# Two of the last four row tiles kept in PSUM, the last softmax in one bank, and a new instruction order

## The chip, the cores and the metric

The kernel runs on one core of a Trainium2 chip. The metric is device time in microseconds (us) of that core; a comparison is between medians of several runs. The profiler takes one execution of the program apart, and its own time is given beside its span.

## What is computed

```python
def reference(A_x, A_wqkv, A_wo, B_x, B_W_gate, B_W_up, B_W_down):
    ...
    x = A_x                                   # 1 x 2048 x 512, bf16
    xn = _layernorm(x, axis=-1)
    return x + _A_ref(xn, A_wqkv, A_wo) + _B_ref(xn, B_W_gate, B_W_up, B_W_down)
```

A is multi-head attention over 2048 tokens with 32 heads of 16 columns: the product with wqkv gives q, k and v, then per head softmax(q k^T / 4) v, then the product with wo. B is a gated layer: (relu(xn W_gate) * (xn W_up)) W_down, with 1792 columns in the middle. The input x is added to the sum of both.

## The kernel before

**Stages.** Queries are taken in four column groups of 512 (`c4` = 0 to 3), heads in four groups of eight (`gg`), and each group of eight in two halves of four heads (`ee`). A block (c4, gg, ee) goes over 16 key tiles of 128. Its raw scores come out of TensorE transposed, keys on the partitions. For most key tiles ScalarE makes the exponential: one unit is an ACTIVATE of 128 x 1024 scores in two PSUM banks (line 1721), and there are 704 units. For the other key tiles ("quads") VectorE, and POOL behind it, build the exponential out of integer arithmetic (lines 1682, 1696, 1699). The weighted sums with v are products into one PSUM bank per block ("PV", `pv_stream`, line 1641); a column of ones in v gives the sum of the exponentials as one more row. `normalise` divides by it: copy out (1544), sums by a small transfer (1562), reciprocal (1583), back by a transfer (1585), spread over the partitions (1597), product (1600).

The gated layer, the projections of q and k and the output rows run between these units as further chains of products (`mm_chain`). An output row tile is 128 tokens x 512 columns: `out_rows` sums the products with W_down (14 pairs) and with wo (one pair per head group) into one bank.

**TensorE's unit of work.** Nearly all products are issued as halves: four matmuls that use 64 of the 128 rows of the array and 32 columns each (`chain_part`, line 1099). Half 0 and half 1 use different rows and can run side by side. Where two halves of one bank follow each other, `follow` (lines 632 to 636) makes the later one wait for the earlier:

```python
if e == "PE" and o.half is not None:
    was = last.get(o.bank)
    if was is not None and was.half != o.half:
        o.deps[was] = True
    last[o.bank] = o
```

**PSUM.** Eight banks: two pairs for the scores of the units (`P_sc`), and four single banks (`P_b`) for everything else: raw scores of quads, PV, row tiles, projections.

**The order.** The order of the instructions on all five queues is written out by hand: `ORDER` (line 154) is a list of the numbers that the instructions get as they are made, and `SLOTS` (line 471) gives the buffers in the same order. `follow` walks both lists, `emit` adds the semaphore waits. Transfers are issued by SP alone, in the order of the list, but for one store that ScalarE issues at the end (`OWN_STORE`).

**The end.** The last four row tiles (c4 = 3, rows 0 to 3) can't wait for the last head group, so `out_rows` sums what is there (14 pairs and two head groups), and VectorE adds x and puts the result into SBUF as fp32 (`resid`, line 1379). The last block (3, 3, 1) is the only one whose PV halves go to two banks (`LAST2` = 1, lines 1612 to 1621), `tp` for half 0 and `tp_hi` for half 1. `normalise_last` (line 1444) then works in two rounds of 256 columns: ScalarE copies `tp` (1471), VectorE adds `tp_hi` (1473), transposes blocks of 32 x 32 (1476) so that the sums lie along a row, takes the reciprocal (1477), transposes it back, broadcast over 32 columns (1478), and multiplies (1480). TensorE meanwhile sums the missing head groups of the four rows into the four score banks (`stream_out`): group 2, the first half of group 3, and, as soon as a round is done, the second half of group 3 (called the finals below). VectorE adds `resid` to rows 0, 1 and 2 while it empties them (1499). For row 3 an fp32 product with an identity matrix (1455) adds `resid` in the bank, and ScalarE empties it (`TAIL_ACT`, 1495). Four stores end the program (1509, 1506).

## Time and profile before

| | before |
|---|---|
| runs: median (lowest to highest of 3) | 672.91 us (672.89 to 673.71) |
| the profiled execution: its own time | 672.07 us |
| the profiled execution: its span | 670.3 us |
| granted TensorE clock, mean | 1.000 |
| DMA: share of the 16 engines' span, main queue | 15.2% |

The span runs from the first to the last instruction of one execution. A row of a group gives line, engine, operation, output and input, shapes and count, then busy time in all and the mean of one in ns, then the idle time of the engine just before these instructions and what ended it. A row of a timeline gives start, length, engine, line and operation, with the number of instructions merged in it, and in brackets the wait before it. Lengths of merged rows run from the first start to the last end. Matmul ends are modelled. PE is TensorE, ACT ScalarE, DVE VectorE, POOL GpSimd, SP SyncE; a q behind the name is the engine's queue of transfers.

### The profile page before, as it was taken

The page shows a single profiled execution, that of the slowest core. Times are in us where ns is not written, and L with a number is a line of the kernel's source. Part 1 is how long each engine was busy: PE and PEld are TensorE (multiplying, and loading weights), DVE is VectorE, ACT ScalarE, POOL GpSimd, SP SyncE. Part 2 cuts the span into 40 slices and gives each one's busy share as a digit, 9 for nine tenths or more (in the row PEclk, how much of TensorE's full clock was granted, in tenths as well). Part 3 has the DMA queues.
Part 4 walks back from the last instruction along what each step waited for, and adds up shares of the span by engine and source line. Part 5 has one row for each costly group of instructions (what it writes and reads, how often), then busy time and mean ns, then how long its engine had stood idle before and what let it go on. Part 6 is the DMA issues. An engine that isn't in the chain of part 4 may idle for free.

```text
span 670.3 us, 44373 instructions
## 1 busy us (share of the span) xinstructions
PE 662.2 (99%) x22332; PEld 368.4 (55%) x19124; DVE 594.4 (89%) x1001; ACT 656.3 (98%) x721; POOL 334.4 (50%) x345
## 2 busy tenths in 40 slices
PE   8999999999999999999999999999999999999997
PEld 3555465555554555555555555555554556565653
DVE  8958899999999888999999788999999967889887
ACT  7999999999999999999999999999999999999995
POOL 3101445555555654564665544664446644545550
PEclk9999999999999999999999999999999999999999
DMA  6530210122320011111100011020200003020101
GB/s 197 82 42 21 53 44 7 37 57 67 93 73 16 6 48 50 35 54 32 29 21 17 10 51 49 21 77 5 61 6 14 9 26 102 21 80 19 29 5 43
DMA packets 51472, 28.66 MB, mean 43 GB/s; under 512 B 18840, under 2 KB 50328, under 8 KB 51288
## 3 DMA queue, kind: packets, MB, share of 16 engines
q1 hardware_dynamic: 51144, 25.70, 15.2%
q8 instruction: 162, 2.65, 1.7%
q14 instruction: 22, 0.18, 0.1%
q10 hardware_dynamic: 144, 0.13, 0.1%
HBM read 18.22 MB, written 2.10 MB: 30 GB/s over the span
## 4 chain that ended last, share of the span: by engine, by line
PE 89%; ACT 7%; DVE 3%; issue 0%; DMA 0%; POOL 0%; DVEq 0%
PE ps L547 88%; ACT ring L1721 7%; DVE stats L1011 1%; DVE qd L1682 0%; DVE xn_sb L1034 0%; DMA x_sb<-in_A_x_dram 0%; DVE xnT L1079 0%; DVE xn_sb L1499 0%; PE ps L1107 0%; DVE x_sb L1600 0%; DVE mv L1013 0%; DVE o_sb L1476 0%; DVE up_sb L1478 0%; DVE o_sb L1473 0%; DVE xnT L1379 0%
## 5 line engine op out<-in xcount | busy, mean ns | idle before, releaser
L1721 ACT ACTIVATE ring<-ps 128x1024 bf16<-128x1024 f32 x704 | 648.3, 1084 | 2.2 <-PE ps L547 1.5
L1696 POOL INT64_ADD qd<-qd x312 | 321.5, 1044 | 290.8 <-DVE qd L1682 142.8
L547 PE MATMUL ps<-qT,kT 64*32 64x512 bf16 x8192 | 462.2, 375 | 1.4 <-ACT ring L1721 0.5
L1682 DVE TENSOR_SCALAR qd<-ps 128x512 int16<-128x512 f32 x640 | 417.4, 686 | 41.8 <-PE ps L547 35.2
L547 PE MATMUL ps<-qd,v_aug 64*32 64x512 bf16 x3840 | 264.7, 375 | 0.0
L547 PE MATMUL ps<-ring,v_aug 64*32 64x512 bf16 x2816 | 228.7, 375 | 0.2 <-issue 0.2
L1661 PEld LDWEIGHTS <-kT 64*32 64x32 bf16 x7332 | 158.6, 92 | 114.5 <-issue 22.8
L1633 PEld LDWEIGHTS <-v_aug 64*32 64x32 bf16 x4308 | 104.0, 92 | 58.3 <-issue 12.0
L547 PE MATMUL ps<-xnT,wus 64*32 64x512 bf16 x1792 | 134.9, 375 | 0.2 <-DVE qd L1682 0.2
L547 PE MATMUL ps<-xnT,wgs 64*32 64x512 bf16 x1792 | 134.4, 375 | 0.0
L547 PE MATMUL ps<-Wd,hT 64*32 64x512 bf16 x768 | 65.5, 375 | 0.0
L1114 PEld LDWEIGHTS <-wgs 64*32 64x32 bf16 x1792 | 43.4, 92 | 30.0 <-issue 6.6
L1114 PEld LDWEIGHTS <-wus 64*32 64x32 bf16 x1792 | 43.5, 92 | 29.1 <-issue 6.2
L1114 PEld LDWEIGHTS <-hT 64*32 64x32 bf16 x1792 | 43.2, 92 | 27.2 <-issue 3.9
L547 PE MATMUL ps<-Wk,hT 64*32 64x512 bf16 x512 | 46.3, 375 | 0.1
L547 PE MATMUL ps<-Wv,hT 64*32 64x512 bf16 x512 | 45.3, 375 | 0.0
L547 PE MATMUL ps<-Wo_p,x_sb 64*32 64x512 bf16 x480 | 41.6, 375 | 0.0
L1335 DVE SCALAR_TENSOR_TENSOR hT<-ps,up_sb 128x512 bf16<-128x512 f32 x56 | 38.2, 683 | 3.5 <-PE ps L547 2.9
L1331 DVE COPY up_sb<-ps 128x512 f32<-128x512 f32 x56 | 38.5, 687 | 3.2 <-PE ps L547 2.9
L547 PE MATMUL ps<-xnT,Wq 64*32 64x512 bf16 x480 | 36.2, 375 | 0.0
L547 PE MATMUL ps<-xnT,Wk 64*32 64x512 bf16 x448 | 33.1, 375 | 0.0
L547 PE MATMUL ps<-Wv,xnT 64*32 64x512 bf16 x512 | 28.1, 375 | 0.5 <-issue 0.3
(83 smaller groups left out, 218.1 us busy)
## 6 DMA issues: line engine op xcount, KB each, us to landing
wus<-in_B_W_up_dram SPq DMA_DIRECT2D x38, 128.0 KB, 2.7
wgs<-in_B_W_gate_dram SPq DMA_DIRECT2D x38, 128.0 KB, 2.8
xr_sb<-in_A_x_dram SPq DMA_DIRECT2D x16, 128.0 KB, 2.6
qT<-qf SPq DMA_DIRECT2D x120, 16.0 KB, 2.4
o_sb<-o_sb SPq DMA_DIRECT2D x60, 32.0 KB, 2.4
out_dram<-xn_sb SPq DMA_DIRECT2D x15, 128.0 KB, 2.4
x_sb<-in_A_x_dram SPq DMA_DIRECT2D x8, 128.0 KB, 2.8
Wd<-in_B_W_down_dram SPq DMA_DIRECT2D x6, 128.0 KB, 3.3
```

The lines of the kernel that those rows point to most:

```text
L547: return e.add_instruction(mybir.InstMatmult(name=e.bass.get_next_instruction_name(), engine=mybir.EngineType.PE, ins=[e.lower_ap(x), e.lo ...
L1011: G.op("DVE", 580, lambda e, m=m: e.bn_stats(stats[:, m, :], xs(m)), reads=[t_xm[m]], writes=[t_st], prio=pr, order=last_xn if m == 4 and ...
L1114: e.ldweights(w()[rows, 32 * j:32 * j + 32], tile_position=(rows.start, 32 * j))
L1331: G.op("DVE", 603, lambda e: e.tensor_copy(up_sb[:, tup.slot, :], bank_of(tu)), reads=[tu], writes=[tup], prio=-590)
L1335: G.op("DVE", 603, lambda e: e.scalar_tensor_tensor(out=hT[:, th.slot, :], in0=bank_of(tg), scalar=0.0, in1=up_sb[:, tup.slot, :], op0=ALU ...
L1633: e.ldweights(vs(j), tile_position=(64 * half, 32 * j))
L1661: e.ldweights(ks(m), tile_position=(64 * half, 32 * m))
L1682: G.op("DVE", 601, lambda e, j=j, tx=tx: e.tensor_scalar(qd[:, tq.slot, 512 * j:512 * j + 512], ps[:, BANK[tx.slot], :], IBIAS[3], 0.0, op ...
L1696: G.op("POOL", POOL_NS, lambda e, x=x, n=n: e.int64_add(x().bitcast(I64), raw().bitcast(I64), SHIFTS[n + 1] * LANES), reads=[ti, tq, t_lib ...
L1721: exp_ops[u] = G.op("ACT", ACT_NS, lambda e, tr=tr, k0=k0: e.activation(ring[:, tr.slot, :, :], ps[:, 4 * k0:4 * k0 + 2, :], ACTF.Exp, sca ...
```

## The change

Rows are made in the order 0, 3, 1, 2. Rows 1 and 2 (`KEEP`) are not emptied by VectorE: their banks (of `P_b`) stay theirs to the end. x is added there by one more pair of the chain, a bf16 identity matrix times the x tile that was loaded for the row (two halves), and the missing head groups are summed into the same bank (`more=6`, and `share`, which hands on the counter that marks the first and the last product of a bank). Their halves need no longer stand behind the last PV. Rows 0 and 3 keep the old way, in one score bank each, and VectorE empties them; ScalarE empties rows 1 and 2 (`TAIL_ACT`), and issues the store of row 2. The fp32 identity product is gone.

The last block's PV goes to one bank (`LAST2` = 0). The softmax transposes this bank in one instruction of 512 columns, takes 16 reciprocals in one, transposes them back in one, and multiplies in two instructions of 256 columns that read the bank. The copies of ScalarE and the additions are gone.

`ORDER` and `SLOTS` are replaced from the third line of `ORDER` on: 8020 instructions in place of 8026. The instructions made ahead of the third row tile keep their numbers; the later ones are shifted by one or two.

```diff
@@ -50,9 +50,10 @@
 POOL_SHARE = 1.0
 POOL1_SHARE = 1.0
 FIRSTD = 2
-LAST2 = 1
+LAST2 = 0
 LASTD = 2
-TAIL_ACT = (3,)
+TAIL_ACT = (1, 2)
+KEEP = (1, 2)
 MUL_SLACK = 2500.0
 PAT_SLACK = 100
 REC_SLACK = 3000
@@ -65,7 +66,7 @@
 XN_WAIT = 0
 SPREAD_NS = 660
 VE_FIRST = True
-OWN_STORE = (3,)
+OWN_STORE = (2,)
 JOB_SHIFT = {2: -1, 6: -4, 9: 3, 13: 4, 14: -1, 33: -1, 34: -4, 36: 2, 41: -2, 47: 1, 49: 4, 50: 1, 51: -4, 53: -1, 59: -9, 71: 2, 72: -4, 73: -1, 75: -2, 78: -2, 79: 3, 80: -1, 83: 5, 84: -4, 88: -1, 89: -1, 92: -1, 97: 4}
 XN_POOL = ()
 XN_NS = 2080
@@ -154,343 +155,342 @@
 ORDER = [
...
-    7791, 7813, 7824, 7978, 7963, 7979, 7971, 7985, 7981, 7994, 7989, 7982, 7986, 7983, 7995, 7987, 7990, 7998, 7999, 8000, 8001, 8002, 8003, 8012, 8013,
-    8014, 8015, 8016, 7996, 7988, 7984, 7997, 7991, 8004, 7992, 8005, 8008, 8017, 8006, 8007, 7993, 8009, 8010, 8011, 8018, 8022, 8019, 8020, 8021, 8023,
-    8024, 8025,
...
+    7988, 7925, 7927, 7698, 7956, 7824, 7992, 7964, 7802, 7700, 7972, 7976, 7979, 7980, 7842, 7843, 7844, 7845, 7990, 7799, 7981, 7999, 7819, 7708, 7993,
+    7996, 7989, 7800, 7983, 7987, 7808, 7701, 7994, 8000, 7717, 7812, 7995, 7820, 7718, 7986, 7795, 7984, 7693, 8001, 8002, 8008, 8004, 7825, 7998, 8007,
+    8009, 8010, 8011, 8012, 8016, 8003, 7985, 7826, 8013, 8005, 8006, 8017, 7822, 7997, 8018, 8019, 7794, 7814, 8014, 8015,
...
@@ -1117,23 +1117,25 @@

         chains = [0]

-        def mm_chain(tile, pairs, reads, prio, sub=0, slots=None, mode="half", weights=None):
+        def mm_chain(tile, pairs, reads, prio, sub=0, slots=None, mode="half", weights=None, more=0, share=None, late=()):

             n = len(pairs)
-            count = [0, n * (2 if mode == "half" else 1)]
+            count = [0, n * (2 if mode == "half" else 1) + more]

             def flags():
                 count[0] += 1
                 return count[0] == 1, count[0] == count[1]
+            if share is not None:
+                share.append(flags)
             made = []
             chains[0] += 1
             for i, (w, x) in enumerate(pairs):
                 at = slots[min(i * len(slots) // n, len(slots) - 1)] if slots else None
                 for half in ((0, 1) if mode == "half" else (None,)):
                     fn, load = chain_part(w, x, lambda: bank_of(tile, sub), half, flags)
-                    G.op("PE", 216, fn, reads=reads, joins=[tile],
+                    G.op("PE", 216, fn, reads=reads + (list(late) if i == n - 1 else []), joins=[tile],
                          prio=prio if prio < 0 else at + BG_PRIO if slots else prio, after=at, mode=mode, half=half, bank=(tile, sub),
-                         load=load, weights=reads if weights is None else weights)
+                         load=load, weights=(reads + (list(late) if i == n - 1 else [])) if weights is None else weights)
                     made.append(G.ops[-1])
             return made

@@ -1346,7 +1348,9 @@

             return xnT[:, i, 0:1024].bitcast(FP32)

-        def out_rows(c4, i, gs, first, last, slots=None, pr=0.0, tile=None, sub=0):
+        kept = {}
+
+        def out_rows(c4, i, gs, first, last, slots=None, pr=0.0, tile=None, sub=0, keep=False):

             t = tile or Tile("ob", P_b, BGBANKS)
             pairs, reads = [], [t_wo]
@@ -1367,6 +1371,12 @@
                 src, rd = xr_sb, [txr]
             else:
                 rd = [t_res[m]]
+            if keep:
+                pairs.append(((lambda: ident[:]), (lambda: xr_sb[:, txr.slot, :])))
+                share = []
+                mm_chain(t, pairs, reads, pr, slots=slots, sub=sub, more=6, share=share, late=[txr, t_id])
+                kept[i] = t, share[0]
+                return
             mm_chain(t, pairs, reads, pr, slots=slots, sub=sub)
             if last:
                 to_ = Tile("ost", P_xn)
@@ -1402,11 +1412,11 @@
         seq, done_h = [], set()
         for c4 in range(NB):
             rows = []
-            for i in range(4):
+            for i in range(4) if c4 < NB - 1 else (0, 3, 1, 2):
                 if c4 < NB - 1:
                     rows.append((upos(c4 + 1) + ROW_AT, RN, lambda s, c4=c4, i=i: out_rows(c4, i, range(4), True, True, slots=s), 2))
                 else:
-                    rows.append((upos(c4 + 1) - 54, RN - 1, lambda s, c4=c4, i=i: out_rows(c4, i, range(2), True, False, slots=s), 2))
+                    rows.append((upos(c4 + 1) - 54, RN - 1, lambda s, c4=c4, i=i: out_rows(c4, i, range(2), True, False, slots=s, keep=i in KEEP), 2))

             todo = [ft for ft in range(0, FT, 2) if (c4, ft) not in done_h]
             both = todo[:(NHS - FT) // 2] if c4 < NB - 1 else []
@@ -1443,62 +1453,47 @@

         def normalise_last(tp, tp_hi):

-            tos = Tile("o", P_o)
-            res_op = {}
             tA, tB = Tile("finA", P_sc, [0]), Tile("finB", P_sc, [1])
-            rows = [(tA, 0), (tA, 1), (tB, 0), (tB, 1)]
+            rows = [(tA, 0), (kept[1][0], 0), (kept[2][0], 0), (tB, 0)]
+            flags = {i: kept[i][1] if i in kept else counted(6) for i in range(4)}
             last = len(G.ops)
             for i in range(4):
                 t, sub = rows[i]
-                if i in TAIL_ACT:
-
-                    o = G.op("PE", 860, lambda e, i=i, t=t, sub=sub: e.matmul(bank_of(t, sub), identf[:], resid(i), start=False, stop=False),
-                             reads=[t_res[12 + i], t_selp], joins=[t], prio=-920, mode="full", after=NU)
-                    res_op[i] = o
                 for n, (tg, wo) in enumerate(((t_oT[(3, 2)], lambda: Wo_p[:, 2, :]), (t_oT[(3, 3)], lambda: Wo_l[:, 0, :]))):
-                    for o in stream_out(t, sub, i, lambda tg=tg, i=i: oT_of(tg)[:, 128 * i:128 * i + 128], wo, [tg], n == 0, False, NU + 5 + i):
-                        o.order |= set(pv_ops[part(keys[-1])][-2:])
+                    for o in stream_out(t, sub, i, lambda tg=tg, i=i: oT_of(tg)[:, 128 * i:128 * i + 128], wo, [tg], n == 0, NU + 5 + i, flags[i]):
+                        if i not in kept:
+                            o.order |= set(pv_ops[part(keys[-1])][-2:])
             tl = Tile("oTl", P_qf)
             oTl = lambda: qf[:, tl.slot, :]
             at_bank = lambda t: ps[:, BANK[t.slot], :]

-            tot, tup = Tile("ot", P_o), Tile("up", P_up)
-            flip = lambda c: o_sb[:, tot.slot, c]
+            tot, tup, tr = Tile("ot", P_o), Tile("up", P_up), Tile()
+            G.op("DVE", 630, lambda e: e.transpose(o_sb[:, tot.slot, :], at_bank(tp)), reads=[tp], writes=[tot], prio=-949)
+            G.op("DVE", 190, lambda e: e.reciprocal(rlast[:], o_sb[:, tot.slot, DH - 1:512:32]), reads=[tot], writes=[tr], prio=-948)
+            G.op("DVE", 630, lambda e: e.transpose(up_sb[:, tup.slot, :], rlast[:].unsqueeze(2).to_broadcast([128, 16, 32])), reads=[tr], writes=[tup], prio=-947)
             half_done, ends = [], []
             for h in range(2):
                 c = slice(256 * h, 256 * h + 256)
-                to, th, tt, tr, ts, tn = (Tile() for _ in range(6))
-                G.op("ACT", 300, lambda e, c=c: e.activation(up_sb[:, tup.slot, c], at_bank(tp)[:, c], ACTF.Copy), reads=[tp],
-                     writes=[th] if h else [tup, th], joins=[tup] if h else [], prio=-950 + h)
-                G.op("DVE", 340, lambda e, c=c: e.tensor_tensor(o_sb[:, tos.slot, c], up_sb[:, tup.slot, c], at_bank(tp_hi)[:, c], ALU.add),
-                     reads=[tp_hi, th], writes=[to] if h else [tos, to], joins=[tos] if h else [], prio=-950 + 10 * h, order=half_done)
-
-                G.op("DVE", 340, lambda e, c=c: e.transpose(flip(c), o_sb[:, tos.slot, c]), reads=[to], writes=[tt] if h else [tot, tt], joins=[tot] if h else [], prio=-949 + 10 * h)
-                G.op("DVE", 190, lambda e, c=c, h=h: e.reciprocal(rlast[:, 8 * h:8 * h + 8], flip(c)[:, DH - 1:256:32]), reads=[tt], writes=[tr], prio=-948 + 10 * h)
-                G.op("DVE", 340, lambda e, c=c, h=h: e.transpose(up_sb[:, tup.slot, c], rlast[:, 8 * h:8 * h + 8].unsqueeze(2).to_broadcast([128, 8, 32])),
-                     reads=[tr, to], writes=[ts], prio=-947 + 10 * h)
-                G.op("DVE", 340, lambda e, c=c: e.tensor_tensor(oTl()[:, c], o_sb[:, tos.slot, c], up_sb[:, tup.slot, c], ALU.mult),
-                     reads=[ts, to], writes=[tn], joins=[tl], prio=-946 + 10 * h)
+                tn = Tile()
+                G.op("DVE", 340, lambda e, c=c: e.tensor_tensor(oTl()[:, c], at_bank(tp)[:, c], up_sb[:, tup.slot, c], ALU.mult),
+                     reads=[tup, tp], writes=[tn], joins=[tl], prio=-946 + 10 * h)
                 half_done = G.ops[-1:]
                 for i in (2 * h, 2 * h + 1):
                     t, sub = rows[i]
                     tf = Tile("fin%d" % i)
-                    if i in res_op:
-                        res_op[i].order.add(fin_prev[(t, sub)])
-                        fin_prev[(t, sub)] = res_op[i]
-                    tf.w += stream_out(t, sub, i, lambda i=i: oTl()[:, 128 * i:128 * i + 128], lambda: Wo_l[:, 1, :], [tn], False, True, -910 + i)
+                    tf.w += stream_out(t, sub, i, lambda i=i: oTl()[:, 128 * i:128 * i + 128], lambda: Wo_l[:, 1, :], [tn], False, -910 + i, flags[i], (1, 0) if i % 2 else (0, 1))
                     t.r += tf.w
                     m = 12 + i
                     to_ = Tile("ost", P_xn)
                     for d in ((slice(0, 512),) if TAIL_ACT or i < 3 else (slice(0, 256), slice(256, 512))):
                         if i in TAIL_ACT:
                             G.op("ACT", 90 + 0.93 * (d.stop - d.start), lambda e, t=t, sub=sub, to_=to_, d=d: e.activation(xn_sb[:, to_.slot, d], bank_of(t, sub)[:, d], ACTF.Copy),
-                                 reads=[tf], writes=[] if to_.w else [to_], joins=[to_] if to_.w else [], prio=-900 + i)
+                                 reads=[tf, t], writes=[] if to_.w else [to_], joins=[to_] if to_.w else [], prio=-900 + i)
                             continue
                         ends.append(to_)
                         G.op("DVE", 70 + 1.04 * (d.stop - d.start), lambda e, i=i, t=t, sub=sub, to_=to_, d=d: e.tensor_tensor(
                             xn_sb[:, to_.slot, d], bank_of(t, sub)[:, d], resid(i)[:, d], ALU.add),
-                             reads=[tf, t_res[m]], writes=[] if to_.w else [to_], joins=[to_] if to_.w else [], prio=-900 + i)
+                             reads=[tf, t, t_res[m]], writes=[] if to_.w else [to_], joins=[to_] if to_.w else [], prio=-900 + i)
                     for k, w in enumerate(to_.w):
                         d = slice(512 // len(to_.w) * k, 512 // len(to_.w) * (k + 1))
                         if i in OWN_STORE:
@@ -1516,20 +1511,22 @@
                     if o.eng == "DVE":
                         o.order.add(half_done[0])

-        def stream_out(t, sub, i, w, wo, reads, start, stop, prio):
+        def counted(n):
+            count = [0]
+
+            def flags():
+                count[0] += 1
+                return count[0] == 1, count[0] == n
+            return flags
+
+        def stream_out(t, sub, i, w, wo, reads, start, prio, flags, halves=(0, 1)):
             made = []
-            for half in range(2):
-                fn, load = chain_part(w, wo, lambda: bank_of(t, sub), half, lambda first=start and not half, last=stop and half: (first, bool(last)))
-                new = not t.w
-                o = G.op("PE", 216, fn, reads=reads + [t_wo, t_wol], writes=[t] if new else [], joins=[] if new else [t], prio=prio, mode="half", half=half,
+            for half in halves:
+                fn, load = chain_part(w, wo, lambda: bank_of(t, sub), half, flags)
+                o = G.op("PE", 216, fn, reads=reads + [t_wo, t_wol], writes=[] if t.w else [t], joins=[t] if t.w else [], prio=prio, mode="half", half=half,
                          bank=(t, sub), after=NU if start else None, load=load, weights=reads)
-                if (t, sub) in fin_prev:
-                    o.order.add(fin_prev[(t, sub)])
-                fin_prev[(t, sub)] = o
                 made.append(o)
             return made
-
-        fin_prev = {}

         def normalise(c4, gg, ee, second):
             tp, tp_hi = pv_tile[(c4, gg, ee, second)]
```

44 lines of the change are left out of this document (22 added, 22 removed), and 619 rows, old and new, of the table ORDER.

## The prediction

> **What bounds the kernel now.** I read the page first (busy times, chain of waits, costliest groups), then the timeline of ScalarE over the whole span, then the timelines of the last 16 us engine by engine, and last the groups and the DMAs of that stretch.
>
> ```profile
> span 670.3 us, 44373 instructions
> PE 662.2 (99%) x22332; PEld 368.4 (55%) x19124; DVE 594.4 (89%) x1001; ACT 656.3 (98%) x721; POOL 334.4 (50%) x345
> ...
> L1721 ACT ACTIVATE ring<-ps 128x1024 bf16<-128x1024 f32 x704 | 648.3, 1084 | 2.2 <-PE ps L547 1.5
> ```
>
> TensorE and ScalarE are both nearly full. The exp row decides: 704 exps fill 648.3 us, one per 648.3 / 704 = 0.921 us, and ScalarE stood idle for 2.2 us before them, 1.5 us of that waiting for scores. Nothing in the change touches an exp, so up to the last exp no order of the instructions can gain more than 2.2 us. The rows of the timeline of ScalarE that show where the 1.5 us lie (start, length, operation, and in brackets the wait before it):
>
> ```profile
> 17.18 21.39 ACT L1721 ACTIVATE ring<-ps 128x1024 bf16<-128x1024 f32 x23 [0.18 <-PE ps L547]
> 38.91 3.77 ACT L1721 ACTIVATE ring<-ps 128x1024 bf16<-128x1024 f32 x4 [0.35 <-PE ps L547]
> 43.10 37.94 ACT L1721 ACTIVATE ring<-ps 128x1024 bf16<-128x1024 f32 x41 [0.41 <-PE ps L547]
> ...
> 208.92 355.80 ACT L1721 ACTIVATE ring<-ps 128x1024 bf16<-128x1024 f32 x386 [0.35 <-PE ps L547]
> 564.91 95.84 ACT L1721 ACTIVATE ring<-ps 128x1024 bf16<-128x1024 f32 x104 [0.19 <-PE ps L547]
> ...
> 654.16 6.59 ACT L1721 ACTIVATE ring<-ps 128x1024 bf16<-128x1024 f32 x7
> ```
>
> Five waits of 0.18 to 0.41 us (mean 0.30). The last exp ends at 654.16 + 6.59 = 660.75; call it E. Behind it come 670.3 - 660.75 = 9.55 us in which no exp runs: that is the stage that the change rebuilds. VectorE and ScalarE in it:
>
> ```profile
> 661.05 0.69 DVE L1379 TENSOR_TENSOR xnT<-ps,xr_sb 128x512 f32<-128x512 f32 x1 [0.92 <-PE ps L547]
> 661.75 0.42 DVE L1473 TENSOR_TENSOR o_sb<-up_sb,ps 128x256 f32<-128x256 f32 x1
> ...
> 663.40 0.42 DVE L1480 TENSOR_TENSOR qf<-o_sb,up_sb 128x256 bf16<-128x256 f32 x1
> 663.74 0.41 DVE L1473 TENSOR_TENSOR o_sb<-up_sb,ps 128x256 f32<-128x256 f32 x1
> ...
> 665.39 0.42 DVE L1480 TENSOR_TENSOR qf<-o_sb,up_sb 128x256 bf16<-128x256 f32 x1
> 665.73 1.88 DVE L1499 TENSOR_TENSOR xn_sb<-ps,xnT 128x512 bf16<-128x512 f32 x3
> ```
>
> ```profile
> 661.23 0.66 ACT L1471 ACTIVATE up_sb<-ps 128x256 f32<-128x256 f32 x2 [0.47 <-PE ps L547]
> 666.96 0.60 ACT L1495 ACTIVATE xn_sb<-ps 128x512 bf16<-128x512 f32 x1 [5.07 <-PE ps L547]
> 667.59 0.40 ACTq L1506 DMA_DIRECT2D out_dram<-xn_sb  x1
> ...
> 666.51 1.46 SPq L1509 DMA_DIRECT2D out_dram<-xn_sb  x3
> ```
>
> and TensorE:
>
> ```profile
> 659.51 0.38 PE L547 MATMUL ps<-qd,v_aug 64*32 64x512 bf16 x4
> 659.52 0.38 PE L547 MATMUL ps<-Wv,hT 64*32 64x512 bf16 x4
> 659.73 0.38 PE L547 MATMUL ps<-qd,v_aug 64*32 64x512 bf16 x4
> 659.74 0.38 PE L547 MATMUL ps<-Wv,hT 64*32 64x512 bf16 x4
> ...
> 660.80 0.82 PE L547 MATMUL ps<-ring,v_aug 64*32 64x512 bf16 x16
> ...
> 663.89 0.38 PE L547 MATMUL ps<-Wo_l,qf 64*32 64x512 bf16 x4
> 664.33 0.39 PE L547 MATMUL ps<-Wo_l,qf 64*32 64x512 bf16 x8
> 664.65 1.12 PE L1455 MATMUL ps<-xnT,identf 128*128 128x512 f32 x2
> 665.71 1.21 PE L547 MATMUL ps<-Wo_l,qf 64*32 64x512 bf16 x20
> ```
>
> The reader should see three things. First, the unit of TensorE's work here is a half: four matmuls of 64 rows. A half starts 0.22 us (659.51, 659.73) after the one before it on the same rows, takes 0.38 us to its end, and one of the other rows runs beside it (659.52): two halves per 0.216 us when the rows alternate. Second, the last PV halves end at 660.80 + 0.82 = 661.62, and then VectorE's softmax sets the pace: first 256 columns ready at 663.82, the other 256 only at 665.39 + 0.42 = 665.81. Third, everything left then follows: four halves of rows 2 and 3 end at 666.92, ScalarE empties row 3 (666.96 to 667.56), VectorE its third row (to 667.61), and the stores close the span.
>
> **The change, part by part.** *Softmax.* Removed: two ScalarE copies and two VectorE additions (0.42 each), since all products of the block are in one bank. Two transposes of 256 columns become one of 512, twice. Rows for the durations:
>
> ```profile
> L1476 DVE STREAM_TRANSPOSE o_sb<-o_sb 128x256 f32<-128x256 f32 x2 | 0.9, 446 | 0.1
> L1480 DVE TENSOR_TENSOR qf<-o_sb,up_sb 128x256 bf16<-128x256 f32 x2 | 0.8, 424 | 0.1
> L1473 DVE TENSOR_TENSOR o_sb<-up_sb,ps 128x256 f32<-128x256 f32 x2 | 0.8, 418 | 0.0
> L1499 DVE TENSOR_TENSOR xn_sb<-ps,xnT 128x512 bf16<-128x512 f32 x3 | 1.9, 682 | 0.0
> L1583 DVE RECIPROCAL rrec<-rsum 128x16 f32<-128x16 f32 x1 | 0.2, 241 | 0.0
> ```
>
> A transpose of 512 is not in the trace. From below: an addition of 512 (682), so 0.68; from above: twice a transpose of 256, 0.89. I take 0.446 + (0.682 - 0.418) = 0.71, the step of the additions from 256 to 512. The start: both halves of the last product now go to one bank, and the second waits for the first. The low half started at about 661.23 - 0.04 - 0.38 = 660.81 (ScalarE's copy was released by its end), so the second starts at 661.23 and ends at 661.61: as late as now. VectorE, which no longer has the addition of L1379 at 661.05 in its way, starts near 661.70. Then 0.71 + 0.24 + 0.71 + 0.42 and four gaps of 0.02: the first 256 columns at 663.83 (now 663.82), the others 0.34 to 0.42 later, 664.2 (now 665.81). So the first part gains nothing and the second is 1.6 us earlier.
>
> The Trainium skill, "VectorE: DVE Perf Modes", Rules for kernel authors, speaks against this: it says to copy PSUM to SBUF first where many operations read it, and its table of costs charges 62 cycles more to an operation that reads PSUM. As an estimate by that page, three reads of PSUM at 0.065 us make the end 0.2 us later. The trace doesn't agree: 418 ns with an operand in PSUM, 424 without.
>
> *TensorE behind the last PV.* Counted in the two order lists: 24 halves and the fp32 product (1.12) now, 36 halves after. Twenty of the 36 need no softmax; alternating they take 20 x 0.108 = 2.2 us from 661.44, to 663.6, and some three waits of 0.1 to 0.2 us where a bank changes rows bring that to about the 663.89 at which the first columns can be used. It hides behind VectorE's 2.1 us; uncovered, each further half would cost 0.108. The other 16, in the order of the list, come out as nine steps of 0.216: the last starts at 663.89 + 8 x 0.216 = 665.62 and ends at 666.00, where now it is 666.92. ScalarE's last row then starts at 666.04 instead of 666.96: 0.92 earlier. Row 3 is complete two steps before, at 665.57, and VectorE empties rows 0 and 3 back to back from about 665.17, 2 x 0.68 to 666.55 instead of 667.61. Removing the fp32 product itself gains nothing: it ran while VectorE made the second 256 columns.
>
> From above: if all 16 went one by one, 15 x 0.216 + 0.38 = 3.62 from 663.89 gives 667.51, 0.6 later than now; two dearer transposes (2 x 0.18) would add 0.4 there too. From below: if the finals of row 2 waited for nothing but the columns at 664.2, six halves of the now nine steps less, about 1.3 earlier. I take 0.9, because the list does alternate the rows.
>
> *Stores.* Still four; ScalarE's queue now has row 2, SP the rows 1, 0 and 3, as soon as each is emptied.
>
> ```profile
> out_dram<-xn_sb SPq DMA_DIRECT2D x3, 128.0 KB, 1.7
> out_dram<-xn_sb ACTq DMA_DIRECT2D x1, 128.0 KB, 2.2
> ```
>
> Landing takes what it takes now, so the end moves with the last emptied row: 0.9 earlier.
>
> *Identity products, residual additions, banks.* Four more halves (0.43 us at pairs), two beside the last exps, two among the 16 above. Two additions of L1379 leave VectorE, which waited 0.92 us for TensorE there: nothing gained. The two kept banks replace the second PV bank of the last block and the bank of the moving row tile, so one bank is left for raw scores at the end, as before.
>
> *The new order.* It reorders the whole program. Of the instructions that both lists have, 1369 of 5557 on TensorE keep their rank, 754 of 970 on VectorE, 100 of 341 on POOL, 35 of 396 transfers on SP, all exps. SP's moves (up to 49 places past other transfers) and POOL's (up to 45) are covered by early loads and by POOL's idle half of the span; uncovered, a late weight tile or pattern would show as a wait of TensorE and then of the exps. The price can only be an exp that waits for its scores. Between two score pairs TensorE has 7.8 halves on average, 0.85 us against 0.921. Gaps with six or more halves of the same rows (1.3 us or more) number 11 now and 22 after, and 13 of the 22 lie in the first 70 units, where there are none now. The worst run, units 29 to 35, has 32 halves on one row group: 32 x 0.216 = 6.91 us against 7 x 0.921 = 6.45, so up to 0.46 us late. The present list already waits 0.35 and 0.41 there, so part of it is not new. From below it is -1.5 (all five waits gone); from above eleven more waits of 0.30, +3.3. I take +0.2.
>
> **The sum.** -0.9 + 0.2 = -0.7 us. Against this execution (672.07 us, span 670.3): 671.4 and 669.6. The median shown, 672.91, stands 0.84 above that execution, so for a median I forecast 672.2.
>
> **The rivals.** *Body waits vanish too.* The order list is new and nothing pins the five waits; with 0.7 to 1.5 us of them gone beside the 0.9 of the tail, 672.91 - 1.6 to - 2.4 = 671.3 to 670.5. Against it: the crowded first 70 units.
>
> *Slower: scores come late in units 6 to 67.* One mechanism: TensorE's other work is bunched ahead of score pairs, ScalarE waits. Three new waits of 0.30 eat the 0.9; from 0.2% loss (1.35 us) it needs 7.5; all eleven additional crowded gaps give 3.3 - 0.9 = +2.4, 675.3. For it: the counts. Against: now only five waits come with eleven such gaps, and most of the new ones are followed by a gap with one or two halves, which two score buffers can absorb.
>
> *The halves serialise.* The final halves alternate between banks that both row groups write, and each change waits for the half before: 0.6 later than now, 673.5. For it: the four last halves now take 0.99 us (665.93 to 666.92) against 0.43 alternating. Against: the list interleaves four banks. The Trainium skill, "PSUM — Partial Sum Buffer", on bank collisions, says that different row tiles cannot access one bank at the same time; the serial end of the present finals agrees with it, and by that rule the one-bank softmax is where such waits would gather.
>
> *The gain does not reach the end.* The stores, not the emptied rows, close the span: four landings that overlap; then 672.9.
>
> **How the numbers follow.** Chances: forecast 0.38, body waits vanish 0.28, slower by late scores 0.22, serial halves 0.08, stores 0.04. What a measurement here can tell from no change is 0.2%, 1.35 us: 671.56 to 674.26. The forecast (-0.1 to -1.6 with the bounds nearest to it) lies inside but for 0.09 of its chance; the second case is faster but for 0.02; of the third all but 0.01 is beyond +1.35; the last two are inside. Faster 0.09 + 0.26 = 0.35, slower 0.21, same 0.44. The range reaches to -2.4 (670.5) and takes in most of the third case: 670.5 to 675.0; the forecast's own range is 671.3 to 672.8.
>
> **What would show it.** Right: last exp near 660.9, one transpose of 512 near 0.71, second 256 columns about 3.4 us after E, ScalarE's last row near E + 5.3 (now E + 6.2), no idle of VectorE before the softmax. Wrong: more than five ScalarE waits before 80 us; single unpaired halves behind the last PV; the span behind the last exp still 9.5 us.

## The result, and the profile after

| | before | after |
|---|---|---|
| median of 22 runs each, on the same chip | 672.76 us | 671.45 us (670.56 to 673.30) |
| ratio, 95% interval | | 0.9983 (0.9976 to 0.9989) |
| the profiled execution: its own time, its span | 672.07, 670.3 us | 671.23, 669.4 us |
| last exp ends (E) | 660.75 | 660.93 |
| from E to the end of the span | 9.55 | 8.47 |

The change gains 1.3 us by the medians and 1.1 us by the ratio (0.7 to 1.6). The page of the changed kernel, and ScalarE's timeline:

```profile
span 669.4 us, 44292 instructions
PE 661.9 (99%) x22346; PEld 367.0 (55%) x19050; DVE 591.0 (88%) x993; ACT 656.8 (98%) x720; POOL 334.6 (50%) x345
...
L1718 ACT ACTIVATE ring<-ps 128x1024 bf16<-128x1024 f32 x704 | 648.8, 1089 | 1.8 <-PE ps L547 1.4
```

```profile
17.10 21.63 ACT L1718 ACTIVATE ring<-ps 128x1024 bf16<-128x1024 f32 x23 [0.24 <-PE ps L547]
38.93 3.84 ACT L1718 ACTIVATE ring<-ps 128x1024 bf16<-128x1024 f32 x4 [0.19 <-PE ps L547]
42.96 86.00 ACT L1718 ACTIVATE ring<-ps 128x1024 bf16<-128x1024 f32 x93 [0.19 <-PE ps L547]
129.25 1.02 ACT L1718 ACTIVATE ring<-ps 128x1024 bf16<-128x1024 f32 x1 [0.28 <-PE ps L547]
130.45 437.30 ACT L1718 ACTIVATE ring<-ps 128x1024 bf16<-128x1024 f32 x475 [0.18 <-PE ps L547]
568.03 92.91 ACT L1718 ACTIVATE ring<-ps 128x1024 bf16<-128x1024 f32 x101 [0.28 <-PE ps L547]
...
654.28 6.65 ACT L1718 ACTIVATE ring<-ps 128x1024 bf16<-128x1024 f32 x7
665.04 0.60 ACT L1490 ACTIVATE xn_sb<-ps 128x512 bf16<-128x512 f32 x1 [4.10 <-PE ps L547]
666.40 0.60 ACT L1490 ACTIVATE xn_sb<-ps 128x512 bf16<-128x512 f32 x1 [0.77 <-PE ps L547]
```

Up to E nothing is won: the waits in brackets are six now and sum to 1.36 us (five and 1.48 before), the exps themselves were busy 0.5 us longer in this execution, and E is 0.18 later. Everything won lies behind E. VectorE there, and TensorE around the last PV halves (`ring,v_aug`), at the first finals and at the last product:

```profile
661.89 0.72 DVE L1471 STREAM_TRANSPOSE o_sb<-ps 128x512 f32<-128x512 f32 x1 [2.38 <-PE ps L547]
662.64 0.25 DVE L1472 RECIPROCAL rlast<-o_sb 128x16 f32<-128x16 f32 x1
662.93 0.71 DVE L1473 STREAM_TRANSPOSE up_sb<-rlast 128x512 f32<-128x512 f32 x1
663.68 0.76 DVE L1478 TENSOR_TENSOR qf<-ps,up_sb 128x256 bf16<-128x256 f32 x2
665.49 1.29 DVE L1494 TENSOR_TENSOR xn_sb<-ps,xnT 128x512 bf16<-128x512 f32 x2 [1.05 <-PE ps L547]
```

```profile
661.03 0.38 PE L547 MATMUL ps<-ring,v_aug 64*32 64x512 bf16 x4
...
661.47 0.38 PE L547 MATMUL ps<-ring,v_aug 64*32 64x512 bf16 x4
...
664.16 0.40 PE L547 MATMUL ps<-Wo_l,qf 64*32 64x512 bf16 x8
...
665.97 0.38 PE L547 MATMUL ps<-Wv,hT 64*32 64x512 bf16 x4
```

All 512 columns are ready at 663.68 + 0.76 = 664.44, 3.51 behind E, where the second 256 were ready 5.06 behind E before. ScalarE's last row starts 5.47 behind E (before 6.21), VectorE's last ends at 666.78, ScalarE's at 667.00, 6.07 behind E (before 6.86). VectorE stands idle for 1.05 us between softmax and rows: TensorE is still at work on row 0. TensorE's last product, for the row that ScalarE empties last, ends at 666.35. Followed back from its end, the chain of work that ended last now stays on TensorE through the whole stage, up to 666.38; before, it ran over VectorE from 661.05 on. TensorE's own products now take about as long as the softmax.

### The profile page after: what moved, and what is told of

Read it like the earlier page. It is cut to its first block, busy times and chain, and to the rows that moved or that the text cites. A ratio compares the mean times of both kernels' runs of the same rounds, so it can differ in the third digit from the quotient of the medians.

```text
span 669.4 us, 44292 instructions
## 1 busy us (share of the span) xinstructions
PE 661.9 (99%) x22346; PEld 367.0 (55%) x19050; DVE 591.0 (88%) x993; ACT 656.8 (98%) x720; POOL 334.6 (50%) x345
## 4 chain that ended last, share of the span: by engine, by line
PE 94%; ACT 4%; DVE 1%; DMA 0%; issue 0%; POOL 0%
PE ps L547 93%; ACT ring L1718 3%; DVE qd L1679 1%; DMA x_sb<-in_A_x_dram 0%; DVE stats L1011 0%; ACT qT L1267 0%; DVE x_sb L1597 0%; PE ps L1241 0%; POOL rstd L995 0%; PE ps L1107 0%; DVE rb L1594 0%; PE ps L1059 0%; ACT xn_sb L1490 0%; DVE hT L1337 0%; DVE xn_sb L1034 0%
## 5 line engine op out<-in xcount | busy, mean ns | idle before, releaser
L1718 ACT ACTIVATE ring<-ps 128x1024 bf16<-128x1024 f32 x704 | 648.8, 1089 | 1.8 <-PE ps L547 1.4
L547 PE MATMUL ps<-ring,v_aug 64*32 64x512 bf16 x2816 | 225.9, 375 | 0.1
L1658 PEld LDWEIGHTS <-kT 64*32 64x32 bf16 x7256 | 155.7, 92 | 114.0 <-issue 20.0
L547 PE MATMUL ps<-xnT,wgs 64*32 64x512 bf16 x1792 | 135.9, 375 | 0.0
```

The source lines that it names most:

```text
L547: return e.add_instruction(mybir.InstMatmult(name=e.bass.get_next_instruction_name(), engine=mybir.EngineType.PE, ins=[e.lower_ap(x), e.lo ...
L1658: e.ldweights(ks(m), tile_position=(64 * half, 32 * m))
L1718: exp_ops[u] = G.op("ACT", ACT_NS, lambda e, tr=tr, k0=k0: e.activation(ring[:, tr.slot, :, :], ps[:, 4 * k0:4 * k0 + 2, :], ACTF.Exp, sca ...
```

## Experiments: where the gain lies

**The seam between body and end.** Four kernels take the order of one kernel up to the score products of a unit U and the rest from the other. In short:

```diff
-ORDER = [the list of the kernel whose end this is]
+ORDER = first + [i for i in that list if i not in first]   # first: the other kernel's list up to unit U
+SLOTS = [...]                                              # assigned anew
```

With U = 650, the body of before and the end of after:

> The instructions of the changed kernel; order of before up to the scores of unit 650 (about 7360 of 8020 instructions), the new order behind that. Theory A (the gain is made behind the last exp: 670.3 - 660.75 = 9.55 us before, 669.4 - 660.93 = 8.47 after): the stage behind the last exp takes 8.5 us, the last exp ends within 0.4 of 660.8, the span is near 669.3, the ratio to before near 0.998. Theory B (the new order of the body brings a good part of the measured 1.1 us): the ratio is 0.9995 or more. Both leave room for a wait of a few tenths at the seam.

Ratio 1.0069 (1.0053 to 1.0085); its profiled execution: span 675.1, E 666.67, stage behind E 8.43. And the reverse:

> The instructions of the kernel before; the new order up to the scores of unit 650, the order of before behind that. Theory A: 9.5 us behind the last exp, last exp within 0.4 of 660.9, ratio to before 1.000 (0.999 to 1.001). Theory B: ratio 0.9985 or less with 9.5 us behind the last exp.

Ratio 1.0035 (1.0023 to 1.0048); E 663.00, stage 9.6. The stages fit a gain that lies in the end; but both kernels are slower than the two that they are made of. ScalarE's timeline of the first says why:

```profile
614.29 4.75 ACT L1725 ACTIVATE ring<-ps 128x1024 bf16<-128x1024 f32 x5 [0.69 <-PE ps L554]
...
632.99 29.44 ACT L1725 ACTIVATE ring<-ps 128x1024 bf16<-128x1024 f32 x32 [0.78 <-PE ps L554]
664.73 1.94 ACT L1725 ACTIVATE ring<-ps 128x1024 bf16<-128x1024 f32 x2 [2.31 <-PE ps L554]
```

Four waits at the seam and behind it (one of 0.23 us at 619.26 is not shown), 4.0 us in all, none of which either kernel has. At unit 650 the two lists differ in what has been done, so work is done too early or too late there; the pair measures its own seam. At U = 640 with the buffers carried over consistently:

> The instructions of the changed kernel once more with the order of before in the body, now joined at the scores of unit 640, where the two lists differ by 4 instructions and every buffer keeps its place over the seam. Theory A (the gain is made behind the last exp): ScalarE waits in the body as before (idle near 2 us before the exps), last exp within 0.4 of 660.8, 8.4 to 8.5 us behind it, span near 669.3, ratio to before 0.998 to 0.999. Theory B (the new order of the body brings a good part): ratio 0.9995 or more.

> The instructions of the kernel before, new order up to the scores of unit 640, order of before behind that, buffers kept over the seam. Theory A: 9.5 to 9.6 us behind the last exp, last exp within 0.4 of 660.9, ratio to before 0.999 to 1.001. Theory B: ratio 0.9985 or less with 9.5 us behind the last exp.

| | ratio to before (95%) | E | stage behind E |
|---|---|---|---|
| body of before, end of after | 0.9989 (0.9975 to 1.0002) | 661.26 | 8.44 |
| body of after, end of before | 0.9995 (0.9982 to 1.0007) | 660.87 | 9.53 |

The rows that give the first stage: E is 654.61 + 6.65, and the last row follows 5.43 behind it, as in the changed kernel.

```profile
654.61 6.65 ACT L1725 ACTIVATE ring<-ps 128x1024 bf16<-128x1024 f32 x7
...
666.69 0.60 ACT L1497 ACTIVATE xn_sb<-ps 128x512 bf16<-128x512 f32 x1 [0.77 <-PE ps L554]
```

The end's 1.1 us go with the order and the code behind unit 640 and not with the body. By the medians neither half is told from no change alone.

**The width of the transposes.** The changed kernel with its softmax in two rounds of 256 columns, in short:

```diff
-transpose 512; reciprocal 16; transpose back 512
 for h in range(2):
+    transpose 256; reciprocal 8; transpose back 256
     multiply 256
```

> The changed kernel, with the softmax of the one bank in two rounds of 256 columns again (transpose, reciprocal, transpose, product, twice). Theory A, by the rows of before: 0.45 + 0.20 + 0.45 + 0.42 and gaps per round, so the first columns 0.6 us earlier than now (near E + 2.6 instead of E + 3.2), the second near E + 4.1 instead of E + 3.5; behind them six steps of 0.216 and 0.38, so ScalarE's last row starts 0.5 later (E + 5.9 instead of E + 5.47) and the stage takes 8.9 to 9.0 us. Rival (the transposes of 512 are no part of the gain, TensorE's 36 halves set the time): the stage stays at 8.4 to 8.5 us.

Ratio 1.0002 (0.9993 to 1.0011). VectorE, then TensorE's first finals, then ScalarE, in its profiled execution (E 660.64):

```profile
662.76 0.42 DVE L1485 TENSOR_TENSOR qf<-ps,up_sb 128x256 bf16<-128x256 f32 x1
...
664.29 0.42 DVE L1485 TENSOR_TENSOR qf<-ps,up_sb 128x256 bf16<-128x256 f32 x1
```

```profile
663.74 0.42 PE L554 MATMUL ps<-Wo_l,qf 64*32 64x512 bf16 x8
```

```profile
666.51 0.60 ACT L1497 ACTIVATE xn_sb<-ps 128x512 bf16<-128x512 f32 x1 [1.27 <-PE ps L554]
```

The first columns are ready 2.54 behind E, earlier than in the changed kernel, the second 4.07 behind E, 0.56 later; the last row starts 5.87 behind E, 0.40 later, and the stage is 8.86 against 8.47. The later columns set the end, not the first: one wide round is worth 0.4 us. The early first columns find no use: they are ready at 663.18, but TensorE is still at the products that need no softmax and starts the first finals at 663.74, 3.10 behind E. In the changed kernel the first finals start at 664.16, 3.23 behind E and 0.06 after their columns (663.68 + 0.42). So TensorE waits for the softmax only some 0.1 us there (3.23 - 3.10): earlier first columns alone could gain no more, an estimate from these two starts.

**Who adds x and empties the kept rows.** The changed kernel without the identity products; VectorE adds x while it empties all four rows. In short:

```diff
-pairs.append((ident, x tile))
-ACT activation(xn_sb, bank, Copy)
+DVE tensor_tensor(xn_sb, bank, x tile, add)
```

> The changed kernel without the two identity products: VectorE empties rows 1 and 2 too and adds x while it does so, so it empties all four rows. Theory A (two rows on each engine are half of the gain): four additions of 0.65 in a row from about E + 4.1 end near E + 6.75 instead of ScalarE's E + 6.07 (667.00 - 660.93), the stage takes 9.0 to 9.2 us, so most of the gain is lost. Rival (only the earlier softmax counts, the stores close the span): 8.5 us.

Ratio 1.0015 (1.0006 to 1.0024), stage 10.24, for a reason of its own: row 1's addition stood in VectorE's queue ahead of the second multiplication, which it held up to 665.87. With these two exchanged in the order:

> As e4_x_by_vector (no identity products, VectorE empties all four rows and adds x), but with VectorE's second product of the softmax ahead of its first row, which there stood in the way of it. Theory A (two rows on each engine are part of the gain): the first product's rows start near E + 4.1, four additions of 0.65 end near E + 6.75 to 6.9 instead of E + 6.07, the stage behind the last exp takes 9.0 to 9.3 us instead of 8.47. Rival (only the earlier softmax counts): 8.5 us.

Ratio 0.9984 (0.9974 to 0.9995); E 660.77, stage 8.83. VectorE:

```profile
663.50 0.75 DVE L1484 TENSOR_TENSOR qf<-ps,up_sb 128x256 bf16<-128x256 f32 x2
664.87 0.69 DVE L1496 TENSOR_TENSOR xn_sb<-ps,xr_sb 128x512 bf16<-128x512 f32 x1 [0.61 <-PE ps L554]
665.48 1.28 DVE L1500 TENSOR_TENSOR xn_sb<-ps,xnT 128x512 bf16<-128x512 f32 x2
666.67 0.68 DVE L1496 TENSOR_TENSOR xn_sb<-ps,xr_sb 128x512 bf16<-128x512 f32 x1
```

Four rows in series end 6.58 behind E; two engines with two rows each end 6.07 behind E. Up to the last emptied row the split is worth 0.51 us; the stage loses only 0.36 without it, less than theory A asked (9.0 to 9.3), because the span closed 2.25 behind the last row for 2.40. Both are net of the identity products: without them TensorE's last product starts 4.82 behind E for 5.04. The medians of two kernels this close can't show either.

**The fp32 product alone.** The kernel before without it, so that row 3 lacks x and the first part of its sum.

```diff
-G.op("PE", 860, ... identf ... resid(3))
```

> The kernel before without the fp32 identity product of row 3, which leaves x and the first part of the sum out of row 3. Prediction's claim (the product ran while VectorE made the second 256 columns, so its removal alone gains nothing): 9.5 us behind the last exp, no change of the ratio (0.9995 to 1.0005). Rival (the product and its change of tile size stand in the chain): up to 1.1 us less, stage 8.4 to 9.0 us, ratio below 0.999.

Ratio 1.0000 (0.9986 to 1.0013), E 662.97, stage 9.53: its removal alone gains nothing, as the prediction said. (E is late in this execution, which took 674.28 us, the second slowest of ten; the edit leaves the order up to E as it was.)

**The width on the kernel before.** Its softmax in one round of 512 columns, with the two banks and the old split of the rows. The fp32 product moves too: it stands ahead of all finals, where before had it in their middle. In short:

```diff
-for h in range(2): copy 256; add 256; transpose, reciprocal, transpose back, multiply 256
+copy 512; add 512; transpose 512; reciprocal 16; transpose back 512
+for h in range(2): multiply 256
```

> The kernel before, with its last softmax in one round of 512 columns instead of two of 256: one copy by ScalarE, one addition, one transpose, one reciprocal of 16, one transpose back, then the two multiplications; TensorE's fp32 product stands ahead of the finals. The rows keep their old split (VectorE rows 0, 1 and 2 in series, ScalarE row 3). Theory A (the width and the split of the rows each carry part of the 1.1 us): the second multiplication ends sooner than before's second round, but VectorE still empties three rows one behind the other, and the copy and the addition now run in series; the stage behind the last exponential stays between 9.2 and 9.6 us (before 9.55), ratio 0.999 to 1.001. Rival (the width alone is the gain): the stage falls to 8.6 us or less and the ratio to 0.998 to 0.999.

Ratio 1.0003 (0.9990 to 1.0015), stage 10.16: above what either theory expected. ScalarE's copy, VectorE and TensorE (E 660.94):

```profile
661.42 0.60 ACT L1476 ACTIVATE up_sb<-ps 128x512 f32<-128x512 f32 x1 [0.48 <-PE ps L553]
```

```profile
662.15 0.69 DVE L1477 TENSOR_TENSOR o_sb<-up_sb,ps 128x512 f32<-128x512 f32 x1 [0.22 <-ACT up_sb L1476]
...
664.65 0.76 DVE L1484 TENSOR_TENSOR qf<-o_sb,up_sb 128x256 bf16<-128x256 f32 x2
666.49 1.89 DVE L1503 TENSOR_TENSOR xn_sb<-ps,xnT 128x512 bf16<-128x512 f32 x3 [1.07 <-PE ps L553]
```

```profile
664.55 1.13 PE L1461 MATMUL ps<-xnT,identf 128*128 128x512 f32 x2
665.62 2.04 PE L553 MATMUL ps<-Wo_l,qf 64*32 64x512 bf16 x32
```

With two banks the wide round must first copy 512 columns and then add them. The columns are ready at 665.41, 4.47 behind E: the second 256 come 0.6 earlier than before, but the first 256 (664.65 + 0.42 = 665.07) come 1.1 later. VectorE's row 0 needs those, and three rows hang on it in series: they start at 666.49, 5.55 behind E instead of 4.98. The stage loses 0.6 us. Most of that isn't the width's: the first finals start at 665.62, when the fp32 product is through, 0.55 behind their columns, where before (663.89 for 663.82) and after have 0.06 to 0.07. An estimate from these rows gives the product's place 0.5 us and the width 0.1. A wide round on two banks with the product in its old place was not run; shown is only that this kernel gains nothing, while the wide round on the single bank, which needs neither copy nor addition, is worth 0.4.

## Experiments: the order of early transfers

In the profiles the early waits of ScalarE (12 to 50 us) differ by order: with the order of before 0.94, 1.95, 1.16, 1.88 and 0.98 us (before, the two bodies of before, the runs without fp32 product and with the wide round), with that of after 0.59 to 0.76 in six. One thing that differs there is SP's queue. Its transposing transfers of the normalised rows (the transposing loads of the expectations), before and after:

```profile
21.50 2.70 SPq L1041 DMA_TRANSPOSE xnT<-xn_sb  x2
24.25 0.58 SPq L1318 DMA_DIRECT2D wus<-in_B_W_up_dram  x1
24.88 3.22 SPq L1041 DMA_TRANSPOSE xnT<-xn_sb  x2
28.15 0.59 SPq L954 DMA_DIRECT2D Wk<-in_A_wqkv_dram  x1
28.78 0.50 SPq L1318 DMA_DIRECT2D wgs<-in_B_W_gate_dram  x1
30.75 6.41 SPq L1041 DMA_TRANSPOSE xnT<-xn_sb  x4
```

```profile
21.95 14.54 SPq L1041 DMA_TRANSPOSE xnT<-xn_sb  x8
```

After has the eight in one merged row, and the profile's list of transfers gives a median of 2.8 us from issue to landing where before has 3.5. The merged row hides a hole. VectorE, then SP, of after:

```profile
29.81 1.05 DVE L1034 TENSOR_SCALAR xn_sb<-hT,mv,rstd 128x512 bf16<-128x512 bf16 x3
```

```profile
30.89 5.60 SPq L1041 DMA_TRANSPOSE xnT<-xn_sb  x4
```

The fourth transfer was through at 28.00, and the fifth left at 30.89, just behind three normalisings of rows (29.81 + 1.05 = 30.86). Before's fifth left at 30.75, so two of its three weight loads (28.15 and 28.78) stood in a hole that is there without them. Three kernels move these transfers alone (instruction numbers, in short; 33 is the rest of Wk, 34 the rest of Wq, 355, 372 and 374 belong to the gated layer, 2645 is an x tile, the others are transposing):

```diff
 SP of before, two variants (transfers in a new order, then in a row)
-34, 152, 148, 372, 150, 154, 33, 374, 175, 181, 179, 177
+33, 34, 154, 150, 148, 152, 181, 179, 175, 177, 372, 374
+33, 34, 152, 148, 150, 154, 175, 181, 179, 177, 372, 374
 SP of after, in the order of before
-33, 2645, 34, 154, 150, 148, 152, 181, 179, 175, 177, 372, 355, 374
+34, 152, 148, 372, 150, 154, 33, 374, 175, 181, 179, 177, 2645, 355
```

> The kernel before, with nothing changed but the order of 11 early transfers on SP's queue, which is taken from the changed kernel: the rest of Wk moves ahead, and the eight transposing loads of x stand one behind the other with no weight load between them. Theory A (this order is what made the early units of the changed kernel wait less): ScalarE's waits between its exponentials before 50 us fall to 0.5 to 0.8 us (the bodies in the old order showed 0.9 to 2.0), the transposing loads land 2.7 to 3.0 us after their issue (old order 3.4 to 3.6), the last exponential ends up to 0.5 us earlier than 660.75, the stage behind it stays 9.5 us, ratio 0.9985 to 1.0. Rival (the order on TensorE and VectorE made it): waits stay 0.9 to 2.0, ratio 0.9995 to 1.0005.

> The changed kernel, with nothing changed but the first 26 transfers on SP's queue, which come in the order of the kernel before (weight loads between the transposing loads of x). Theory A: ScalarE's waits before 50 us rise from 0.6 to between 0.9 and 2.0 us, the transposing loads land 3.4 to 3.6 us after their issue, the last exponential ends 0.3 to 1.3 us later than 660.93, the stage behind it stays 8.5 us, ratio to the kernel before 0.9985 to 1.0. Rival: waits stay near 0.6, the ratio stays that of the changed kernel, 0.998.

Both came out slower: 1.0079 (1.0060 to 1.0098) and 1.0038 (1.0024 to 1.0052). VectorE's normalising, SP and ScalarE of the first, then of the second:

```profile
24.40 0.40 DVE L1041 TENSOR_SCALAR xn_sb<-hT,mv,rstd 128x512 bf16<-128x512 bf16 x1
```

```profile
24.83 12.82 SPq L1048 DMA_TRANSPOSE xnT<-xn_sb  x8
```

```profile
33.24 1.02 ACT L1728 ACTIVATE ring<-ps 128x1024 bf16<-128x1024 f32 x1 [2.23 <-PE ps L554]
```

```profile
23.87 0.73 DVE L1041 TENSOR_SCALAR xn_sb<-hT,mv,rstd 128x512 bf16<-128x512 bf16 x2
```

```profile
24.63 2.89 SPq L1048 DMA_TRANSPOSE xnT<-xn_sb  x2
```

```profile
32.92 2.05 ACT L1725 ACTIVATE ring<-ps 128x1024 bf16<-128x1024 f32 x2 [1.68 <-PE ps L554]
```

In both the first transposing transfer starts some 3 us late (24.83 for 21.50, 24.63 for 21.95), and with it everything behind it on the queue. The two lists normalise the rows of x in different orders on VectorE: before has those of load 152 ahead of those of 154 (places 184 and 233), after the reverse (237 and 193). Each kernel's transfers follow its own order of rows. Put in the other's, the transfer that stands first is the one whose rows come last of the first four. The rows show it: these rows are ready at 24.80 (24.40 + 0.40) and 24.60 (23.87 + 0.73), and the transfer leaves 0.03 us later. ScalarE's waits before 50 us sum to 4.40 and 3.08 us. So these two runs don't tell whether the weight loads between cost anything; they price a queue whose head isn't ready. E goes to 665.67 and 664.07, that is 4.9 and 3.1 later. (The second's stage is 8.83: its rows end 6.05 behind E as in the changed kernel, and the span closes 0.4 later behind them.) The third keeps the order of rows and moves only the weight loads away:

> The kernel before, with the eight transposing loads of x in the order it gave them, the one whose rows are ready first standing first, but with no weight load between them: the rest of Wk goes ahead of them, the two loads of the gated layer behind them. Theory B (the weight loads between them hold them up, and the first needs only to be ready): the first transposing load starts near 21.5 us as before, they land 2.7 to 3.1 us after their issue, ScalarE's waits between 12 and 50 us come to 0.5 to 0.8 us (the bodies in the old order showed 0.9 to 2.0), the last exponential ends 0.1 to 1.0 us earlier than in these, ratio 0.9985 to 1.0. Rival (the weight loads between them cost nothing; the order of rows on the engines makes the difference): the waits stay at 0.9 to 2.0 us and the ratio at 0.9993 to 1.0010.

Ratio 0.9977 (0.9966 to 0.9987): 1.5 us faster than the kernel before by the ratio (0.9 to 2.3), 1.2 by the medians (671.34 for 672.53), with its old end and without the change. Its profiled execution doesn't show where:

```profile
7.64 1.29 SPq L961 DMA_DIRECT2D Wk<-in_A_wqkv_dram  x1
...
21.54 15.66 SPq L1048 DMA_TRANSPOSE xnT<-xn_sb  x8
```

```profile
41.07 21.19 ACT L1728 ACTIVATE ring<-ps 128x1024 bf16<-128x1024 f32 x23 [1.75 <-PE ps L554]
```

Waits of 1.93 us, landing 3.4 us, E 661.40: theory B's rows failed, and only its total came, more than it asked. But that execution took 672.72 us, the slowest of the twelve, the others 670.60 to 672.42. A wait of 1.75 us that the others may not have is in it. That the new order of these transfers gains is shown by the times; by which wait is not, and that it is the row of transposing transfers isn't either. In this execution the fifth left at 30.79 and the last was through at 37.20, where before has 30.75 and 37.16; only the third and the fourth left 0.4 to 0.5 us earlier. The same edit brings the rest of Wk 20 us forward (7.64 for 28.15) and puts the two loads of the gated layer 9 and 13 us back, and no run takes these apart.

## Why the prediction was right, and where it wasn't

**The time.** 671.45 us lies in the forecast's own range, 0.75 below its 672.2, and by the ratio (0.17%) within the 0.2% that it called no difference, though 0.1 below its band in us (671.56), since before's median is 672.76 now; the interval still excludes no change. Profiled against profiled, 672.07 became 671.23: -0.84 for the -0.7 of the sum. Most of the 0.75 is no matter of the kernels: the forecast set the new median 0.84 above its profiled execution, as before's was, and it stood 0.22 above.

**The end, -0.9: right in its mechanism, measured -1.08.** The order of events was as worked out: first columns no earlier, second ones far earlier (3.51 behind E, predicted 3.4), transposes of 512 at 0.72 and 0.71 (predicted 0.71), ScalarE's last row 5.47 behind E (5.3), removal of the fp32 product worth nothing. The last PV ended 0.92 behind E (predicted 0.86, "as late as now"), the softmax started 0.96 behind (predicted 0.95). One sign that it named failed: VectorE did stand idle ahead of the softmax, for 2.38 us, which costs nothing, since it waited for the last PV.

The step that was mis-sized is the chain of products behind the softmax: nine steps of 0.216 from the first columns were to end 5.25 behind E and ended 5.42 behind (666.35). Half of the difference is its start, 3.23 behind E for 3.14, the other half its pace, eight steps in 1.81 us for 1.73. The rows as emptied therefore gained 0.79 (6.86 to 6.07) and not 0.9. The other 0.29 came where the prediction had put nothing, "landing takes what it takes now": from the last emptied row to the end of the span it was 2.69 before and 2.40 after (ScalarE's store landed in 1.9 us for 2.2). Over the other runs this last piece was 2.64 to 2.72 with the old end and 2.25 to 2.41 with the new one, but once 2.78 there, so that part is less certain.

Taken out one at a time, the wide round costs the stage 0.39 us (0.40 up to the last emptied row) and two rows per engine 0.36 (0.51). Up to the last row these are more than the 0.79 together, so they overlap and don't add up. What the single bank is worth by itself was not run.

The Trainium skill, "VectorE: DVE Perf Modes", Rules for kernel authors, leaves a choice for work on PSUM: accept its rate, or copy it to SBUF first if many operations follow. The runs speak against the copy here: the transpose of 512 took 0.72 us out of PSUM and 0.71 out of SBUF, so nothing pays for the 0.60 us of a copy of 512 columns. The kernel that copies first (the wide round on the kernel before) has its columns ready 4.47 behind E, the changed one 3.51; part of that is the addition of the second bank, 0.69 us.

**The body, +0.2: the number came in one execution, by luck; the reason didn't.** E is 0.18 later in the profiled execution, which the medians can't resolve: the body alone, with the end of before, stands at 0.9995 (0.9982 to 1.0007), -0.3 us by the middle (-1.2 to +0.5). And the step behind it said that units 29 to 35 would be up to 0.46 us late, from the count of crowded gaps. The waits there fell: 0.19 and 0.19 for 0.35 and 0.41. The count of halves of one row group in a gap doesn't price a wait. What made up for the smaller waits in this execution is the exps' busy time, 648.8 for 648.3; over the profiles of both orders it runs from 648.1 to 649.1, so it isn't the order's.

**"SP's moves are covered by early loads": not so.** Eleven early transfers in another order cost 5 us, and moving three weight loads out from between the transposing ones gained 1.5. Moves of a few places on this queue count. The new order, whose head fits its own order of rows, shows no such cost.

**The rivals.** Body waits did not vanish (1.36 us of 1.48 stayed). Late scores in units 6 to 67 did not come: three waits before 80 us, three before the change. Halves serialise at the last PV, at 0.44 us for a step; single halves, named as a sign of being wrong, do stand behind it (starts at 663.20, 663.43 and 663.65), but the finals still went in nine steps. The stores followed the last emptied row.

**Open.** Which wait the third order of transfers removes, whether by the row of transposing ones or by the earlier Wk, and why the changed kernel, which has both too, doesn't show that gain in its body. That order of transfers and the changed end together, which beside each other gain 1.5 and 1.1, were not run in one kernel.

## What to carry to other kernels

Read the end of a kernel from the last instruction of its bottleneck engine on: up to the last emptied row that stage was the same to 0.1 us whatever the body did (6.03 to 6.07 with the new end, 6.85 to 6.95 with the old), and it alone resolved gains of 0.4 us. In a serial softmax look at when the last part is ready, not the first: one wide pass beat two narrow ones on the single bank, and earlier first columns were worth nothing while the engine that takes them was busy. Before a run is read as the price of one part, look whether another part moved with it, as the fp32 product did in the wide round on the kernel before. An in-order transfer queue has to follow the order in which its sources are made; look at when the head's source is ready before moving anything, because a few places can cost or gain more than the change itself.

## What the runs showed of the hardware

- A transpose of 32 x 32 blocks on VectorE takes 0.45 us for 256 columns of fp32 and 0.71 to 0.72 for 512, with its source in PSUM or in SBUF alike: two narrow ones cost 0.18 us more than a wide one.
- The same 704 exps were busy 648.1 to 649.1 us in the profiled executions of kernels that don't differ in them.
- A transposing transfer held SP's queue for 1.2 to 2.8 us and landed 2.8 to 3.6 us after its issue by the median of the eight; a weight load among them took 0.5 to 0.6 us of the queue.
- The transfer at the head of SP's queue left 0.03 us after VectorE had made its rows (24.83 for 24.80, 24.63 for 24.60), and those behind it waited with it.
